# A two-layer gated network behind chunked attention on one core: some loads spread out, some stores moved from SP's queue to POOL's

## The chip, the cores and the metric

The kernel runs on one core of a Trainium2 chip. The metric is the device time of one execution in microseconds (us); the median of the timed runs counts. TensorE (PE) multiplies, VectorE (DVE), ScalarE (ACT) and GpSimd (POOL) work on tiles in SBUF, and SyncE (SP) issues DMA transfers. POOL and ACT can issue transfers too. Each engine takes its instructions strictly in the order of the program, and an instruction whose operand isn't there holds up all that stand behind it on that engine.

## What is computed

Attention over chunks of 64 tokens (8 batches, 8 heads, 576 tokens, 64 per head), whose result is laid out as x with 4608 tokens of 512, and then two gated layers with weights of 512 x 1536, 512 x 1536 and 1536 x 512; the second normalises its input first.

```python
def _moe_ref(x, w_gate, w_val, w_out):
    g = x @ w_gate
    silu = g * (1.0 / (1.0 + np.exp(-g)))
    val = x @ w_val
    return (silu * val @ w_out).astype(np.float32)

def _moe2_ref(x, w_gate, w_val, w_out, rms_g):
    rms = np.sqrt(np.mean(x * x, axis=-1, keepdims=True) + 1e-06)
    xn = x / rms * rms_g
    ...                          # then as above, on xn
```

## The kernel before

**Precision.** Every factor is split into a high part and a low rest, and a product is three matmuls: high by high, high by low, low by high (`mm3`, L641). The weights come as 64-bit numbers and are turned to 32 bits on ACT and DVE.

**Plain blocks.** The first layer's first 2560 tokens go through in five blocks of 512 (`emit_g`, `emit_v`, `emit_y`, j = 0 to 4), each in 12 iterations f over the hidden width; (j, f) names one. In block j the chunks run upwards or downwards by turns, so that the last three of a block are the first of the next. An iteration is 12 matmuls of g, 12 of v and 12 of the y of the iteration before. The weights' high parts stay in SBUF, their low parts don't: all but a few are stored to `lo1_d` in block 0, and blocks 1 to 4 load them again, `load_lo` (L193, tile l, 512 KB, g and v together, three slots) two iterations ahead and `load_lo_o` (L200, tile lo, 256 KB).

**Positions.** An iteration has three positions, numbered through from block 0; (j, f) begins at 36 j + 3 f. `put` (L805) hangs a step on a position and `spread` (L808) cuts a list of transfers into n nearly equal pieces on n positions in a row. On the positions hang the attention of the next tokens (tile i from position `score_at(i)` on; POOL normalises p, `att_n` L533, then DVE transposes it, `att_td` L541), the loads of q and k in 13 groups of 32 small transfers (`load_qk` L352; DVE transposes a piece of them in `trans_att` L457), the first layer's weight sums (`whole`, `first_add`, `first_keep`, L268 to L301: POOL adds in block 1 to 4, SP stores to `w1_d`) and the second layer's weight products (`comb_add`, `comb_cast`, `comb_rest`, `comb_keep`, L216 to L256: POOL and ACT work, SP stores to `w2_d`). `later2` names the ten of the 18 products that are made only in the tail.

**The tail.** From the end of block 4 on, seven stages s of up to 2 x 512 tokens (s = 0 and 1 the first layer's last 2048 tokens, s = 2 to 6 the second layer) use a scheme of seven products for a 2 x 2 block product. A stage is a gv stretch (6 x 14 products, six matmuls each) and a y stretch (42 products, six matmuls each). Their weights pass through a ring of 16 slots in SBUF: `load_ring` (L952) issues loads up to a number, each as soon as its slot is free. In s = 0 and 1 the ring tiles with k > 2 are loaded as one full number; `ring_split` (L973) makes the high part on ACT (L982) and the low on DVE or POOL (L985). The first ring loads are issued inside block 4, `load_ring(4)` at the start of (4, 8) and `load_ring(16)` at the start of (4, 9), ahead of what these iterations load themselves.

**Queues.** SP issues all transfers but eight, in program order: a load of l stands behind every q, k, v, weight, store and ring transfer that the program names before it.

Of the kernel before, what the change touches and what calls it, by code (L numbers as in the profile page):

```python
# [9 lines left out]
F32 = mybir.dt.float32  # L10
# [9 lines left out]
def tile_kernel(  # L20
# [14 lines left out]
    lo1_d: bass.AP,  # L35
    w1_d: bass.AP,
    x1_d: bass.AP,
    out: bass.AP,
):
    nc = tc.nc  # L40
# [44 lines left out]
    NB = TAIL // NW  # L85
# [94 lines left out]
    def chunk(j, f):  # L180
        return f if j % 2 == 0 else NF - 1 - f
# [68 lines left out]
    def comb_keep(nm, fp, k):  # L250
        z = SLOT[k]
        w = comb[1, nm, fp]["w", z // 2]
        a = z - z % 2
        nc.sync.dma_start(
            out=w2_d["gvo".index(nm), fp, :, a:z + 1], in_=w[:, :z - a + 1].bitcast(F32)
        )  # L256

# [37 lines left out]
        nc.gpsimd.tensor_tensor(out=t[which], in0=a, in1=b, op=op)  # L295

    def first_keep(nm, p, side):
        nc.sync.dma_start(
            out=w1_d["gvo".index(nm), p, :, 3 + 2 * side:5 + 2 * side],
            in_=flat[0, nm, 2 * p + side].rearrange("p (k f) -> p k f", k=2),  # L300
        )  # L301

    def place(nm, k):
        return {3: 6, 5: 4 if nm == "o" else 5, 4: 3, 6: 5 if nm == "o" else 4}[k]
# [29 lines left out]
    groups = [list(range(0, 2 * EARLY - 2)), list(range(2 * EARLY - 2, 2 * EARLY))]  # L334
# [122 lines left out]
    def trans_att(i):  # L457
        ts_ = []
        for z, nm in enumerate("qk"):
            t = att.tile([P, HP, P], F32, tag=f"{nm}T", name=f"{nm}T{i}")  # L460
            tv = t.rearrange("p a (b c) -> p a b c", c=32)
            (g0, n0), (g1, n1) = where[2 * i], where[2 * i + 1]
            if g0 == g1:
                nc.vector.transpose(out=tv, in_=gt[g0][z][:, :, 2 * n0:2 * n0 + 4, :])
            else:
                nc.vector.transpose(out=tv[:, :, 0:2], in_=gt[g0][z][:, :, 2 * n0:2 * n0 + 2, :])
                nc.vector.transpose(out=tv[:, :, 2:4], in_=gt[g1][z][:, :, 2 * n1:2 * n1 + 2, :])
            ts_.append([t[:, hp] for hp in range(HP)])
        qkT[i] = ts_
# [335 lines left out]
    def put(l, j, pos, fn):  # L805
        at.setdefault((l * NB + j) * NP + pos, []).append(fn)
# [12 lines left out]
    def score_at(i):  # L819
        return NP + 9 * (i - 8) // 2  # L820

    turned = {}
    for i in range(NW // P, NT_):
        j = order[i] * P // NW
        if i >= 8:
            a = score_at(i)
            m_, t_, n_, d0, d1 = ((1, 2, 3, 6, 8), (1, 3, 3, 5, 7))[i % 2]
            if i == 8:
                put(0, 0, a - 1, lambda: trans_att(8))
            put(0, 0, a, lambda i=i: att_both(i))  # L830
            put(0, 0, a + m_, lambda i=i: att_m(i))
            if i + 1 < NT_:
                put(0, 0, a + t_, lambda i=i: trans_att(i + 1))
                turned[i + 1] = a + t_
            put(0, 0, a + n_, lambda i=i: att_n(i))
            put(0, 0, a + d0, lambda i=i: att_td(i, 0))
            put(0, 0, a + d1, lambda i=i: att_td(i, 1))
            e = score_at(i + 2)
            if i + 2 >= NT_:
                put(0, 0, e, lambda i=i: att_both(i + 2))  # L840
            put(0, 0, e + 1, lambda i=i, j=j: att_lo(i, j))
        else:
            b = 9 * (i - 4)
            late = i == 4
            put(0, 0, b + (2, 1, 0, 0)[i - 4], lambda i=i: trans_tok(i))
            put(0, 0, b + 2 + late, lambda i=i: att_s(i))
            put(0, 0, b + 3 + late, lambda i=i: att_m(i))
            put(0, 0, b + 4 + late, lambda i=i: att_n(i))
            put(0, 0, b + 6 + late, lambda i=i: att_t(i))
            put(0, 0, b + 7 + late, lambda i=i, j=j: att_pv(i, j))  # L850
            put(0, 0, b + 8 + late, lambda i=i, j=j: att_lo(i, j))
        for c in (2 * i, 2 * i + 1):
            g = where[c][0]
            if g > 0 and c == groups[g][-1] and g + 2 < len(groups):
                if i > 8:
                    dq, nq = turned[i] + 1, 7
                else:
                    dq, nq = {4: (20, 9), 6: (29, 8), 8: (38, 7)}[i]
                spread(0, 0, dq, nq, lambda g=g: load_qk(g + 2))
    for j in range(1, NB):  # L860
        pj = j - 1
# [23 lines left out]
    w2 = [(nm, f) for nm, fp in pairs2[:8] for f in (fp, fp + NP2)]  # L885
    later2 = pairs2[8:]
# [24 lines left out]
    for j, p, nm in w1_at:  # L911
        a = 3 * min(chunk(j, 2 * p), chunk(j, 2 * p + 1)) + (3 if nm == "o" else 0)
# [39 lines left out]
    def load_ring(n):  # L952
        nonlocal wnext
        while wnext < min(n, len(wseq)):
            s, m, fp, k = wseq[wnext]
            t = wraw.tile([P, 2, HK], F32R, tag=RING[wnext % len(RING)], name=f"wr{m}{fp}_{k}_{s}")
            z = "gvo".index(m)
            if s >= NS:
                nc.sync.dma_start(out=t.bitcast(F32), in_=w2_d[z, fp, :, SLOT[k]])
            elif k > 2:  # L960
                nc.sync.dma_start(out=t[:, 1].bitcast(F32), in_=w1_d[z, fp, :, place(m, k)])
            else:
                side, c = PLAIN[m][k]
                nc.sync.dma_start(out=t[:, 0].bitcast(F32), in_=w1_d[z, fp, :, k])
                nc.sync.dma_start(
                    out=t[:, 1].bitcast(F32), in_=lo1_d[2 * fp + side, :, z, c * HK:(c + 1) * HK]
                )
            wt[s, m, fp, k] = t
            wnext += 1

    wsn = [0, 0]

    def ring_split(n):  # L973
        for z in range(2):
            while wsn[z] < min(n + 2 - 2 * z, wnext, len(wseq)):
                s, m, fp, k = wseq[wsn[z]]
                wsn[z] += 1
                if s >= NS or k < 3:
                    continue
                t = wt[s, m, fp, k]  # L980
                if z == 0:
                    nc.scalar.copy(t[:, 0], t[:, 1].bitcast(F32))  # L982
                else:
                    eng = nc.gpsimd if wsn[z] > 36 and m == "v" else nc.vector
                    eng.tensor_sub(t[:, 1], t[:, 1].bitcast(F32), t[:, 0].bitcast(F32))  # L985

    xo = {}
    xf = {}
# [395 lines left out]
    with tc.manual_schedule():  # L1384
        nc.vector.memset(ones.bitcast(F32), 1.0)
        make_identity(nc, ident)
        w1 = [(nm, f) for f in range(NF) for nm in "gvo"]
# [102 lines left out]
        for n, (l, j, f) in enumerate(iters):  # L1490
            def run(p):
                for fn in at.get(3 * n + p, ()):
                    fn()
                for kt, op in XFIRST.get(3 * f + p, ()) if j == NB - 1 else ():
                    xops[kt][op]()

            head = (l, j) == (0, 0)
            if (j, f) == (1, 0):
                conv.close()
                cv = open_pool(conv, "cv2", 2, "right")  # L1500
            if (j, f) == (NB - 1, 8):
                conv.close()
                attn.close()
                X2 = open_pool(two, "x2", 1, "right")
                for kt in range(2):
                    x_load(0, kt)
                    xops[kt] = x_prep(0, kt)
            if (j, f) == (NB - 1, 8):
                load_ring(4)

            if head and f == 0:
                pre_w1(8)
                issue(later)
                pre_w1(9)
                issue(load_tok(5))
            if head and f == 4:
                nc.sync.dma_start(out=rg, in_=moe2_rms_g.rearrange("(c p) -> p c", p=P))
            if head and f in (2, 5):
                issue(load_tok(6 + f // 5))
            if (j, f) == (NB - 1, 9):  # L1520
                load_ring(16)
            if prev is not None:
                lo()
            sg, product = emit_g(l, j, f)
            run(0)
            if head:
                conv1(3 * f + 4 if f else 2)
            v_product, lo = emit_v(l, j, f, sg)
            product()
            run(1)  # L1530
            if head and f == 0:
                conv1(3)
                conv1(4)
            elif head:
                conv1(3 * f + 5)
            if prev is not None:
                emit_y(*prev)
            v_product()
            if prev is not None and prev[2] == NF - 1:
                evac_y(*prev[:2])  # L1540
            run(2)
            if head:
                if not f:
                    conv1(5)
                conv1(3 * f + 6)
            prev = (l, j, f)
# [40 lines left out]
        for s in range(len(SB)):  # L1587
# [39 lines left out]
            for n in range(0, len(items), 2):  # L1627
                kk, fp = items[n]
# [62 lines left out]
```

## Time and profile before

| | us |
|---|---|
| three timed runs: median (lowest to highest) | 1735.5 (1734.0 to 1736.37) |
| the profiled execution | 1733.73 |
| its span, first to last instruction | 1731.8 |
| PE busy in it | 1695.7 (98%) |
| DVE, ACT, POOL busy | 1200.8, 865.8, 519.1 |
| the five plain blocks end at | 594.7 |
| the tail s = 0, 1, 2 begins at | 594.7, 771.6, 949.1 |

Busy times are of one profiled execution. Matmuls overlap in their pipeline, so a busy PE isn't a PE at its best pace; a stage's length against that of a like stage tells more. A line of waits names the engine and the line that stood idle, and what ended it. SPq is SP's queue: its instructions are issues, and the time of one is not that of the transfer.

### The profile page before, as it was taken

To read this page: it belongs to the slowest core of one execution; us is meant where nothing else is said; L and a number is where in the kernel's file an instruction comes from. 1 tells how busy PE (TensorE), PEld (TensorE's weight loads), DVE (VectorE), ACT (ScalarE), POOL (GpSimd) and SP (SyncE) were. 2 spreads that over 40 slices of the span, in tenths; PEclk is the share of its full clock that TensorE was granted. 3 is DMA by queue.
4 is the path that set the end of the run, shared out by engine and by line. 5 is a ranking of instruction groups with operands and counts; after the bars stand their busy time and mean duration, and the time that the engine had idled before them with its cause. 6 is when DMAs were issued, how large, how long until landed. Compare 5 with 4: busy or idle time off the path is not lost.

```text
span 1731.8 us, 29672 instructions
## 1 busy us (share of the span) xinstructions
PE 1695.7 (98%) x9870; PEld 1431.2 (83%) x9870; DVE 1200.8 (69%) x1936; ACT 865.8 (50%) x2044; POOL 519.1 (30%) x513
## 2 busy tenths in 40 slices
PE   7999999999999999999999999999999999999998
PEld 5788887877788788878887888888888888999998
DVE  6996767866664687896889477833783477358356
ACT  6774544545443466665665455433543354345343
POOL 1004657657563347227723541000000000000000
PEclk9999999999999999999999999999999999999999
DMA  9997888878888678746775799886788678989986
GB/s 237 321 256 171 212 217 246 215 210 247 210 263 284 197 223 282 228 138 218 239 241 157 244 322 307 223 215 194 239 223 215 194 230 230 272 271 284 278 253 175
DMA packets 486806, 405.98 MB, mean 234 GB/s; under 512 B 279552, under 2 KB 362752, under 8 KB 486656
## 3 DMA queue, kind: packets, MB, share of 16 engines
q1 hardware_dynamic: 483456, 403.71, 80.2%
q8 instruction: 79, 1.29, 0.3%
q10 hardware_dynamic: 3200, 0.39, 0.1%
q14 instruction: 71, 0.58, 0.1%
HBM read 321.91 MB, written 82.05 MB: 233 GB/s over the span
## 4 chain that ended last, share of the span: by engine, by line
PE 79%; DMA 7%; DVE 7%; SPq 3%; issue 1%; ACT 1%; POOL 1%; DVEq 0%; POOLq 0%; ACTq 0%
DMA l<-lo_scratch 2%; PE g L644 2%; SPq L453 2%; PE g L642 2%; PE g L643 2%; PE v L642 2%; PE ygA L643 2%; PE yvA L643 2%; PE yvA L644 2%; PE ygA L644 2%; PE yvA L642 2%; PE ygA L642 2%; PE v L643 2%; PE v L644 2%; DVE hp L1162 1%
## 5 line engine op out<-in xcount | busy, mean ns | idle before, releaser
L1126 POOL TENSOR_TENSOR h<-h,h 128x512 f32<-128x512 f32 (+1 forms) x42 | 56.7, 1351 | 661.5 <-DVE h L1104 661.5
L1162 DVE TENSOR_TENSOR hp<-h,hp 128x512 fp32r<-128x512 f32 (+1 forms) x252 | 164.6, 678 | 23.8 <-ACT hp L1161 18.6
L1161 ACT CAST hp<-h 128x512 fp32r<-128x512 f32 (+1 forms) x252 | 140.8, 589 | 41.2 <-PE yvA L644 13.0
L1085 ACT ACTIVATE sgt<-sgt 128x512 f32<-128x512 f32 (+1 forms) x126 | 75.9, 602 | 162.2 <-DVE sgt L1092 162.1
L644 PE MATMUL g<-xh,l 128*128 128x512 f32 x240 | 96.5, 402 | 14.9 <-DMA l<-lo_scratch 14.8
L535 POOL TENSOR_TENSOR p<-p,r 128x512 f32<-128x512 f32 x36 | 40.9, 1137 | 213.4 <-DVE r L534 177.6
L1104 DVE TENSOR_TENSOR h<-h,sgt 128x512 f32<-128x512 f32 (+1 forms) x126 | 89.1, 707 | 15.4 <-ACT sgt L1085 3.2
L642 PE MATMUL g<-xh,wg 128*128 128x512 f32 x240 | 95.5, 398 | 1.6 <-ACT xh L616 1.0
L642 PE MATMUL v<-xh,wv 128*128 128x512 f32 x240 | 96.3, 401 | 0.7 <-ACT wo L167 0.7
L643 PE MATMUL g<-xl,wg 128*128 128x512 f32 x240 | 95.2, 397 | 0.4 <-DVE xl L636 0.4
L644 PE MATMUL v<-xh,l 128*128 128x512 f32 x240 | 94.1, 392 | 0.0
L643 PE MATMUL v<-xl,wv 128*128 128x512 f32 x240 | 94.0, 392 | 0.0
L654 ACT ACTIVATE sg<-g 128x512 f32<-128x512 f32 x60 | 35.8, 596 | 92.4 <-PE g L644 91.8
L655 DVE SCALAR_TENSOR_TENSOR sg<-sg,g 128x512 f32<-128x512 f32 x60 | 41.0, 683 | 55.3 <-ACT sg L654 54.8
L644 PEld LDWEIGHTS g<-xh,l 128*128 128x128 f32 x240 | 46.1, 192 | 28.3 <-DMA l<-lo_scratch 18.4
L507 ACT ACTIVATE p<-both,m 128x64 f32<-128x64 f32 x224 | 66.7, 323 | 1.1
L643 PE MATMUL ygA<-hp,wro 128*128 128x512 f32 (+1 forms) x168 | 63.2, 376 | 0.4 <-DVE hp L1162 0.4
L642 PE MATMUL ygA<-hp,wro 128*128 128x512 f32 (+1 forms) x168 | 63.0, 375 | 0.4 <-ACT s3g L1078 0.4
L642 PE MATMUL yvA<-hp,wro 128*128 128x512 f32 (+1 forms) x168 | 62.8, 374 | 0.0
L644 PE MATMUL ygA<-hp,wro 128*128 128x512 f32 (+1 forms) x168 | 62.7, 373 | 0.0
L643 PE MATMUL yvA<-hp,wro 128*128 128x512 f32 (+1 forms) x168 | 62.7, 373 | 0.0
L644 PE MATMUL yvA<-hp,wro 128*128 128x512 f32 (+1 forms) x168 | 62.7, 373 | 0.0
(846 smaller groups left out, 5465.9 us busy)
## 6 DMA issues: line engine op xcount, KB each, us to landing
wrg<-w_scratch SPq DMA_DIRECT2D x210, 256.0 KB, 3.2
wrv<-w_scratch SPq DMA_DIRECT2D x210, 256.0 KB, 3.1
wro<-w_scratch SPq DMA_DIRECT2D x210, 256.0 KB, 3.4
l<-lo_scratch SPq DMA_DIRECT2D x36, 512.0 KB, 5.7
wrg<-w_scratch SPq DMA_DIRECT2D x84, 128.0 KB, 3.1
wrv<-w_scratch SPq DMA_DIRECT2D x84, 128.0 KB, 3.1
wro<-w_scratch SPq DMA_DIRECT2D x84, 128.0 KB, 2.4
lo<-lo_scratch SPq DMA_DIRECT2D x40, 256.0 KB, 4.5
```

What stands on the lines that cost most here:

```text
L507: nc.scalar.activation(pt[:, hp, x], s3[:, x, hp], AF.Exp, scale=SCALE, bias=m[:, x, hp:hp + 1], accum_out=r[:, 2 * hp + x],)
L535: nc.gpsimd.tensor_tensor(out=p8, in0=p8, in1=r.to_broadcast([P, HP * 2, CH]), op=ALU.mult)
L642: nc.tensor.matmul(o, sh, mh, start=first, stop=False, skip_group_check=free)
L643: nc.tensor.matmul(o, sh, ml, start=False, stop=False, skip_group_check=free)
L644: nc.tensor.matmul(o, sl, mh, start=False, stop=last, skip_group_check=free)
L654: nc.scalar.activation(sg[:, :n], g[:, :n], AF.Tanh, scale=0.5)
L655: return sg, lambda: nc.vector.scalar_tensor_tensor(out=sg[:, :n], in0=sg[:, :n], scalar=1.0, in1=g[:, :n], op0=ALU.add, op1=ALU.mult)
L1085: nc.scalar.activation(t[:, :tw], src[:, :tw], AF.Silu)
L1104: nc.vector.tensor_mul(h[:, :tw], src[:, :tw], sgt[pos][:, :tw])
L1126: nc.gpsimd.tensor_sub(a, a, b)
L1161: nc.scalar.copy(hh[:, :tw], src)
L1162: nc.vector.tensor_sub(hl[:, :tw], src, hh[:, :tw].bitcast(F32))
```

## The change

- `comb_keep` stores of the eight products made in the plain blocks are issued by POOL; those in `later2` stay with SP. `first_keep` stores are all issued by POOL. Together 32 + 36 transfers.
- The loads of q and k: where a group's pieces lay on 7 positions, they lie on up to 10, as far as the first transpose that reads them allows (9 groups; those at 48, 89 and 129 keep 7); the group at 38 begins at 37 and takes 8.
- `load_ring` in block 4 goes to 6, 11 and 16 at the start of (4, 9), (4, 10) and (4, 11).
- A new scratch `l1_d` in DRAM: in s = 0 the low halves of w_out's tiles with k > 2, which DVE has just made, are stored by SP, two calls of `ring_split` later; in s = 1 SP loads them beside the full numbers, and DVE's 24 subtractions fall away.

```diff
 def comb_keep(nm, fp, k):
-        nc.sync.dma_start(
+        queue = nc.sync if (nm, fp) in later2 else nc.gpsimd
+        queue.dma_start(
             out=w2_d["gvo".index(nm), fp, :, a:z + 1], in_=w[:, :z - a + 1].bitcast(F32)
 def first_keep(nm, p, side):
-        nc.sync.dma_start(
+        nc.gpsimd.dma_start(
...
+    STEPS = ((1, 2, 3, 6, 8), (1, 3, 3, 5, 7))
+    def turned_at(i):
+        return score_at(i - 1) + STEPS[(i - 1) % 2][1]
...
                 if i > 8:
-                    dq, nq = turned[i] + 1, 7
+                    first = groups[g + 2][0] // 2
+                    dq = turned_at(i) + 1
+                    nq = min(10, turned_at(first) - dq - 1)
                 else:
-                    dq, nq = {4: (20, 9), 6: (29, 8), 8: (38, 7)}[i]
+                    dq, nq = {4: (20, 9), 6: (29, 8), 8: (37, 8)}[i]
...
             elif k > 2:
-                nc.sync.dma_start(out=t[:, 1].bitcast(F32), in_=w1_d[z, fp, :, place(m, k)])
+                kept = s and m == "o"
+                nc.sync.dma_start(out=t[:, 0 if kept else 1].bitcast(F32), in_=w1_d[z, fp, :, place(m, k)])
+                if kept:
+                    nc.sync.dma_start(out=t[:, 1].bitcast(F32), in_=l1_d[fp, :, place(m, k) - 3])
...
     def ring_split(n):
+        now = lows[:]
+        lows.clear()
+        for age, dst, src in now:
+            if age:
+                nc.sync.dma_start(out=dst, in_=src)
+            else:
+                lows.append((1, dst, src))
...
+                kept = s and m == "o"
                 if z == 0:
-                    nc.scalar.copy(t[:, 0], t[:, 1].bitcast(F32))
-                else:
+                    nc.scalar.copy(t[:, 0], t[:, 0 if kept else 1].bitcast(F32))
+                elif not kept:
                     eng = nc.gpsimd if wsn[z] > 36 and m == "v" else nc.vector
                     eng.tensor_sub(t[:, 1], t[:, 1].bitcast(F32), t[:, 0].bitcast(F32))
+                    if m == "o":
+                        lows.append((0, l1_d[fp, :, place(m, k) - 3], t[:, 1].bitcast(F32)))
...
-            if (j, f) == (NB - 1, 8):
-                load_ring(4)
+            if j == NB - 1 and f >= 9:
+                load_ring((6, 11, 16)[f - 9])
...
-            if (j, f) == (NB - 1, 9):
-                load_ring(16)
```

## Rows read from the trace of the kernel before

**Rows 1.** Stages (from:to length): PE, PEld, DVE, ACT, POOL busy (count), clock, DMA share, GB/s.

```profile
138.10:246.10 108.00, 108.00 (x883) 88.08 (x882) 77.57 (x130) 54.35 (x201) 63.55 (x66) 1.00 0.82 202
246.10:361.20 115.10, 109.83 (x947) 88.91 (x946) 81.73 (x134) 56.46 (x208) 70.95 (x75) 1.00 0.85 225
361.20:482.00 120.80, 113.99 (x948) 90.83 (x947) 82.07 (x138) 57.26 (x210) 72.84 (x78) 0.97 0.82 217
482.00:594.70 112.70, 108.55 (x755) 88.10 (x754) 65.08 (x100) 44.73 (x134) 46.96 (x46) 0.97 0.82 264
...
888.50:949.10 60.60, 59.13 (x254) 46.73 (x253) 57.03 (x101) 38.69 (x81) 14.23 (x5) 1.00 0.53 157
...
1064.30:1121.50 57.20, 57.20 (x254) 47.36 (x253) 52.02 (x84) 30.56 (x55) 1.68 (x1) 1.00 0.81 230
```

**Rows 2.** Who PE waited for: 246 to 595 us, block 2, block 3 (total, times, longest).

```profile
PE g L644 <- DMA l<-lo_scratch: 14.8, 6, 4.1
...
PE g L644 <- DMA l<-lo_scratch: 4.6, 2, 3.6
...
PE g L644 <- DMA l<-lo_scratch: 6.0, 3, 3.3
```

**Rows 3.** PE in order of time around iteration (4, 11): start, length in us.

```profile
578.11 0.39 PE L642 MATMUL y_b<-hh,wo 128*128 128x512 f32 x1
...
579.47 0.39 PE L642 MATMUL g<-xh,wg 128*128 128x512 f32 x1
...
584.23 0.79 PE L644 MATMUL g<-xh,l 128*128 128x512 f32 x1 [4.14 <-DMA l<-lo_scratch]
...
588.66 0.63 PE L642 MATMUL v<-xh,wv 128*128 128x512 f32 x1
...
592.01 0.39 PE L642 MATMUL y<-hh,wo 128*128 128x512 f32 x1
```

**Rows 4.** SP's issues in order of time, 397 to 417 us: first, moved stores, last.

```profile
398.36 0.81 SPq L453 DMA_DIRECT2D xk<-in_k_dram  x2
...
402.22 0.52 SPq L254 DMA_DIRECT2D w_scratch<-wsg  x1
...
403.31 1.31 SPq L298 DMA_DIRECT2D w_scratch<-wao  x2
...
412.69 0.39 SPq L254 DMA_DIRECT2D w_scratch<-wsg  x1
...
416.12 0.50 SPq L197 DMA_DIRECT2D l<-lo_scratch  x1
```

**Rows 5.** The moved stores in blocks 2 and 3: count, ns min/median/max of an issue.

```profile
L254 SPq DMA_DIRECT2D w_scratch<-wsg x20: 332/408/1377, 250.0 to 459.6; - x20
...
L298 SPq DMA_DIRECT2D w_scratch<-wao x12: 376/393/1598, 250.5 to 467.6; - x12
L298 SPq DMA_DIRECT2D w_scratch<-wav x6: 350/376/523, 308.9 to 375.9; - x6
L298 SPq DMA_DIRECT2D w_scratch<-wag x4: 376/414/1262, 291.8 to 358.8; - x4
```

**Rows 6.** Issue to landing of the l loads in blocks 2 and 3.

```profile
DMA to landing us min/median/max: 4.4/5.8/9.3
```

**Rows 7.** SP's issues in order of time, first and last ring issue of 27.

```profile
561.54 0.32 SPq L964 DMA_DIRECT2D wrg<-w_scratch  x1
...
576.42 0.43 SPq L965 DMA_DIRECT2D wrv<-lo_scratch  x1
```

**Rows 8.** DVE's subtractions of w_out's low halves, s = 1's y stretch.

```profile
L985 DVE TENSOR_TENSOR wro<-wro x24: 412/416/1436, 895.4 to 945.3; 128x256 fp32r<-128x256 f32 x24
```

**Rows 9.** POOL normalising p, and who waited for it (138 to 595 us).

```profile
L535 POOL TENSOR_TENSOR p<-p,r x17: 1041/1045/1441, 243.6 to 478.8; 128x512 f32<-128x512 f32 x17
...
DVE pT L547 <- POOL p L535: 2.9, 1, 2.9
```

**Rows 10.** What ACT waited for, 138 to 595 us.

```profile
ACT wsg L242 <- DMA w_scratch<-wsg: 25.8, 8, 5.3
```

More of the change, by code (lines that the diff above doesn't have):

```diff
@@ L37, in tile_kernel @@
     x1_d: bass.AP,
+    l1_d: bass.AP,
     out: bass.AP,
@@ L820, in score_at @@
         return NP + 9 * (i - 8) // 2
-    turned = {}
+    STEPS = ((1, 2, 3, 6, 8), (1, 3, 3, 5, 7))
+    def turned_at(i):
+        return score_at(i - 1) + STEPS[(i - 1) % 2][1]
     for i in range(NW // P, NT_):
@@ L826, in tile_kernel @@
             a = score_at(i)
-            m_, t_, n_, d0, d1 = ((1, 2, 3, 6, 8), (1, 3, 3, 5, 7))[i % 2]
+            m_, t_, n_, d0, d1 = STEPS[i % 2]
             if i == 8:
@@ L833, in tile_kernel @@
                 put(0, 0, a + t_, lambda i=i: trans_att(i + 1))
-                turned[i + 1] = a + t_
             put(0, 0, a + n_, lambda i=i: att_n(i))
@@ L971, in tile_kernel @@
     wsn = [0, 0]
+    lows = []
     def ring_split(n):
+        now = lows[:]
[5 more added lines that the diff above has]
+                lows.append((1, dst, src))
         for z in range(2):
@@ L1681 @@
             w1 = dp.tile([3, 6, 128, 7, 256], F32, name="w1_scratch")
+            l1 = dp.tile([6, 128, 4, 256], F32, name="l1_scratch")
             x1 = dp.tile([512, 2048], F32, name="x1_scratch")
@@ L1686 @@
                 outs.append(nc.dram_tensor(f"out_{i}_dram", shape, dt, kind="ExternalOutput").ap())
-            tile_kernel(tc, *args, xn, w2, lo1, w1, x1, *outs)
+            tile_kernel(tc, *args, xn, w2, lo1, w1, x1, l1, *outs)
     r = _run(nc, [arrays], core_ids=[0])
```

## The prediction, made before the result was known

> **What bounds the kernel now.** The page's busy table comes first; it only says that TensorE (PE) leads by far, so a change can win no more than what PE loses in some stage. The second view, the table by stage, says where [rows 1]. The three middle plain blocks hold the same matmuls (block 1 two small attention groups fewer), yet take 108.0, 115.1 and 120.8 us: blocks 2 and 3 lose up to 7.1 + 12.8 = 19.9 us against block 1. The y stretch of a tail stage takes 60.6 us for s = 1 and 57.2 for s = 2: 3.4 us lost. From s = 2 on PE is busy all of the stretch, and nothing is to be had.
>
> The third view, who PE waited for from block 2 to the end of block 4, gives one name: the load of a low half, l<-lo_scratch, 14.8 us in 6 waits; 4.6 of it lie in block 2 and 6.0 in block 3 [rows 2]. The fourth, PE in order of time, shows what one such wait costs. In iteration (4, 11) the third matmul of g came 4.14 us late, and from it on a matmul took (588.66 - 584.23) / 10 = 0.44 us where (579.47 - 578.11) / 6 = 0.227 is usual: while PE stood, its granted clock had fallen from 2.4 to 1.2 GHz. The twelve matmuls of g ran 9.19 us instead of 2.72, those of v 3.35 instead of 2.72, so this wait cost 6.5 + 0.6 = **7.1 us** [rows 3]. Blocks 2 and 3 lose 4.6 + 6.0 = 10.6 us in the other waits, and block 3's granted clock of 0.97 adds 0.03 x 120.8 = 3.6: **14.2 us** that have a name, of the 19.9 by difference.
>
> Why is the load late? SP issues nearly every transfer, in the order of the program. Up to the l load before the worst wait of block 3 (3.3 us) SP made 30 issues without a rest, from 398.36 to 416.62: 18.3 / 30 = 0.61 us each [rows 4], against medians of 0.38 to 0.41 for one issue [rows 5]. The l load reached its turn at 416.12 and needs 5.8 us to land, the median [rows 6]. So the queue in front of it was long. Of the 30 issues, 4 are stores that now go to POOL and 21 are pieces of q and k.
>
> **The change part by part.**
>
> (1) *Stores to POOL.* 32 stores of weight products and 36 of first-layer sums leave SP; in blocks 2 and 3 these are 20 + 22 = 42 [rows 5], and 42 x 0.61 = 26 us of SP's queue. If every wait of PE goes, SP has 14 to 20 us less for the rest; 26 is more, so the queue is looser than now even with PE at full pace. Before the worst wait it is 4 x 0.61 = 2.4 us.
>
> (2) *q and k pieces over 10 positions.* A group is 32 issues. At position 121, where the l load of (3, 6) is issued, the group that starts at 116 had put out 6/7 of them (27) and will have put out 6/10 (19): 8 x 0.61 = 4.9 us earlier, with (1) 7.3 us against a wait of 3.3. For (2, 4), position 79, it is 22 against 16, 3.7 us, and stores on top, against a wait of 3.6. Only the group at 129 keeps its 7 positions in block 3, so (3, 10) and (3, 11) get the stores alone; at 42 in 236 us some four in the 22 us before, 2.4 us, against waits of 2.7 together. Something is left there. The pieces end later, but by the table of positions still 3 positions (9 us) or more ahead of the transpose that reads them, where the groups that stay have 2.
>
> Of the 14.2 us with a name (19.9 at most) I take **14** back: what (3, 11) and a wait or two on the edge keep, I set against the part of the 19.9 that has no name. Ends: 6, if bursts in the queue remain, and 19.9.
>
> (3) *Ring loads in steps 6, 11, 16.* Until now 8 ring issues in (4, 8) and 16 in (4, 9) stood ahead of the l load of (4, 11); now 10 do. SP made 27 issues, ring and others, from 561.54 to 576.85, 0.57 each [rows 7]: 14 fewer are 7.9 us, against a wait of 4.1. The wait goes, and the clock's fall with it: **7.1 us**. Ring tiles 11 to 15 will be issued near 578; the first is read 11 tiles of 6 x 0.227 us after the tail's start, at 594.7 + 15 = 610: nothing becomes late there.
>
> (4) *Low halves of w_out kept for s = 1.* In s = 1's y stretch 24 subtractions of 0.416 us go [rows 8], 10 us of DVE's 57.0 in 60.6 [rows 1]. DVE has no reserve there, so I take **2.4** of the 3.4 back; ends 0 and 3.4. For it SP issues 24 stores of 128 KB in s = 0 and 24 more loads in s = 1. The y stretch uses the DMA engines at 0.53 [rows 1] and ring loads run 16 tiles, 22 us, ahead, so they cost nothing; with that cover gone 48 x 0.4 = 19 us.
>
> (5) *What POOL pays.* No row shows POOL issuing a transfer. The nearest are SP's issues of the same stores, 0.33 to 1.6 us [rows 5], and POOL's own instruction over a 128x512 tile, 1.04 [rows 9]. I take 1.0, since it is POOL that has to carry it out. POOL is free for 115.1 - 71.0 + 120.8 - 72.8 = 92 us in blocks 2 and 3 [rows 1]; 42 us fit. The stores stand on POOL behind the tensor ops that made their data, so they wait for little. Behind them stands the normalising of p, which DVE transposes next; that has once been thin, DVE waited 2.9 us for p [rows 9]. I charge **1.5 us**; ends -1 (a gain, since ACT waited 25.8 us for stores to free their buffer, and they leave earlier [rows 10]) and 4.
>
> **Sum:** 14 + 7.1 + 2.4 - 1.5 = 22.0 us. The profiled execution took 1733.7 us (span 1731.8), so one like it would take 1711.7. It was 1.8 faster than the median of the three timed runs, 1735.5; the median comes to **1713.5**.
>
> **The rivals.** *B: the transfers are late, not the queue.* The DMA engines are busy 0.85 and 0.82 of blocks 2 and 3 [rows 1]. If the l loads wait for them, the moved stores still fly on the same engines and the 14 us shrink. For it speaks that an issue took 0.61 us where 0.4 is usual; against it, that block 1, with a share of 0.82, loses nothing. Parts (3) and (4) remain: 7.1 + 2.4 - 1.5 = 8.0, **1727.5**; with some of the 14, down to 1721. The Trainium skill, page "DMA: Bandwidth & Descriptors", section "Issuing engines are not separate DMA queues", states this rival as a rule: transfers started by any engine run on the same 16 DMA engines and interleave, and several issuers save only the time of issuing. By that page part (1) would free 42 x 0.4 = 17 us of SP's queue and not 26, an estimate.
>
> *C: POOL becomes the late engine (slower).* Place: the normalising of p in blocks 2 and 3. POOL's price X for a store decides: 92 us for 42 stores are 2.2 us each; above that POOL falls behind, p comes late, DVE stands at its transposes and PE at the scores. The kernel is slower than before once 42 x (X - 2.2) > 23.5, X = 2.76; at X = 3 it takes 1735.5 - 23.5 + 34 = **1746**. Against it: SP's longest issue of such a store is 1.6 us [rows 5].
>
> *D: no gain.* The l loads are late because their slots come free late, and what one load gains the next loses: 1735, within 0.2%. Against it: SP had no rest ahead of the worst wait [rows 4].
>
> **How the numbers follow.** Forecast 0.58 (own range 1706 to 1721), B 0.24 (1721 to 1731), C 0.08, D 0.07, and 0.03 for more than the forecast (all 19.9 come back). The range 1705 to 1731 holds the forecast and B, some 0.8. A measurement of this kernel tells 0.2%, 3.5 us, from no change: faster 0.58 + 0.24 + 0.03 = 0.85, same 0.07, slower 0.08.
>
> **What would show it.** Right: blocks 2 and 3 near 109 us each; PE waiting under 3 us for l loads; no half clock in (4, 11); s = 1's y stretch near 58 us; POOL's issues near 1 us. Wrong: l loads late with SP at rest (D); l loads landing later than 5.8 us after their issue (B); DVE waiting for p (C); DVE's transposes of q and k waiting for their pieces, which would say that (2) went too far.

## The result, and the profile after

| | before | after |
|---|---|---|
| timed runs: median (lowest to highest), us | 1735.9 (1734.0 to 1739.9), 4 runs | 1706.3 (1705.5 to 1709.1), 4 runs |
| the profiled execution, and its span | 1733.7, 1731.8 | 1709.1, 1707.3 |
| PE waiting for l loads in blocks 2 to 4 | 14.8, 6 times | 2.6, once |
| POOL busy | 519.1 | 549.8 |

The changed kernel is faster by 29.6 us: the ratio is 0.983, 95% interval 0.981 to 0.985. Two of all the timed runs below took far longer than their fellows (3426.9 us, part (4) alone; 4359.2 us, the stores of x on ACT) and are in no median here (with its one the latter's is 1718.4). The changed kernel's stages, as in [rows 1] (from:to length; PE, PEld, DVE, ACT, POOL busy; clock, DMA share, GB/s): blocks 1 to 4, then the y stretches of s = 1 and s = 2.

```profile
137.72:245.77 108.05, 108.05 (x883) 88.13 (x882) 78.07 (x130) 54.24 (x201) 71.00 (x81) 1.00 0.80 206
245.77:354.76 108.99, 108.99 (x948) 89.06 (x946) 86.87 (x134) 56.23 (x208) 82.03 (x96) 1.00 0.90 243
354.76:468.30 113.54, 110.91 (x948) 90.13 (x946) 88.12 (x138) 58.62 (x213) 83.12 (x99) 0.98 0.90 230
468.30:573.74 105.44, 105.44 (x756) 86.26 (x754) 68.16 (x99) 42.26 (x128) 52.40 (x58) 1.00 0.85 273
...
867.12:924.24 57.12, 57.12 (x253) 47.33 (x252) 52.93 (x77) 38.40 (x81) 14.50 (x8) 1.00 0.73 222
1039.50:1096.62 57.12, 57.12 (x254) 47.33 (x252) 51.93 (x84) 30.56 (x55) 1.67 (x1) 1.00 0.82 230
```

Against [rows 1]: blocks 2 and 3 fall from 235.9 to 222.5 (13.4 less), block 4 from 112.7 to 105.4 (7.3), s = 1's y stretch from 60.6 to 57.1 (3.5). That is 24.2 of the 24.5 us between the two spans. In block 2, block 4 and both y stretches PE is now busy from end to end; only block 3 still loses something. One line of the waits from 246 to 595 us says what (total, times, longest), and PE in order of time says where (start, length):

```profile
PE g L646 <- DMA l<-lo_scratch: 2.6, 1, 2.6
```

```profile
455.81 0.39 PE L645 MATMUL g<-xl,wg 128*128 128x512 f32 x1
458.83 0.50 PE L646 MATMUL g<-xh,l 128*128 128x512 f32 x1 [2.63 <-DMA l<-lo_scratch]
...
459.93 0.63 PE L644 MATMUL g<-xh,wg 128*128 128x512 f32 x1
...
462.49 0.63 PE L644 MATMUL v<-xh,wv 128*128 128x512 f32 x1
462.92 0.51 PE L645 MATMUL v<-xl,wv 128*128 128x512 f32 x1
463.27 0.39 PE L646 MATMUL v<-xh,l 128*128 128x512 f32 x1
```

This is iteration (3, 11): a wait of 2.6 us, and behind it 3 us in which matmuls follow each other at 0.43 us: from 459.90 to 462.90 the granted clock is 0.50, which is 1.2 GHz, until 2.4 GHz is back. It is the pattern of [rows 3], which itself is gone from (4, 11). POOL's issues of the moved stores in blocks 2 and 3 (count; ns min/median/max):

```profile
L256 POOL DMA_DIRECT2D w_scratch<-wsg x19: 537/577/608, 245.9 to 435.8; - x19
...
L300 POOL DMA_DIRECT2D w_scratch<-wao x11: 539/548/597, 245.3 to 442.8; - x11
```

### The profile page after: what moved, and what is told of

Read it like the earlier page. It is cut to its first block, busy times and chain, and to the rows that moved or that the text cites. A ratio compares the mean times of both kernels' runs of the same rounds, so it can differ in the third digit from the quotient of the medians.

```text
span 1707.3 us, 29702 instructions
## 1 busy us (share of the span) xinstructions
PE 1685.3 (99%) x9870; PEld 1428.5 (84%) x9870; DVE 1210.6 (71%) x1912; ACT 865.9 (51%) x2044; POOL 549.8 (32%) x581
## 4 chain that ended last, share of the span: by engine, by line
PE 92%; DVE 4%; DMA 2%; ACT 1%; issue 1%; SPq 0%; POOL 0%; DVEq 0%
PE v L644 3%; PE g L646 3%; PE g L644 3%; PE g L645 3%; PE v L645 3%; PE v L646 3%; PE yvA L645 2%; PE ygA L645 2%; PE yvA L646 2%; PE ygA L644 2%; PE yvA L644 2%; PE ygA L646 2%; PE y L644 2%; PE y L645 2%; PE y L646 1%; PE y_b L646 1%
## 5 line engine op out<-in xcount | busy, mean ns | idle before, releaser
L1147 POOL TENSOR_TENSOR h<-h,h 128x512 f32<-128x512 f32 (+1 forms) x42 | 56.7, 1351 | 661.5 <-DVE h L1125 661.5
L678 DVE TENSOR_TENSOR hl<-sg,hh 128x512 fp32r<-128x512 f32 x60 | 61.7, 1029 | 9.3 <-ACT hh L676 8.6
L676 ACT CAST hh<-sg 128x512 fp32r<-128x512 f32 x60 | 37.1, 618 | 54.8 <-DVE sg L673 54.8
L646 PE MATMUL yvA<-hp,wro 128*128 128x512 f32 (+1 forms) x168 | 62.8, 374 | 0.0
L644 PE MATMUL yvA<-hp,wro 128*128 128x512 f32 (+1 forms) x168 | 62.7, 373 | 0.0
```

What stands on the lines that cost most here:

```text
L644: nc.tensor.matmul(o, sh, mh, start=first, stop=False, skip_group_check=free)
L646: nc.tensor.matmul(o, sl, mh, start=False, stop=last, skip_group_check=free)
L678: return product, lambda: nc.vector.tensor_sub(hl[:, :n], sg[:, :n], hh[:, :n].bitcast(F32))
L1147: nc.gpsimd.tensor_sub(a, a, b)
```

## The experiments

Medians are of timed runs; each ratio is to runs of the kernel before beside it. Stages are of one profiled execution. A gain in us beside a ratio, for the four parts, is the ratio taken of 1734.3. 29 runs of the kernel before, beside the first four experiments, lay between 1730.1 and 1742.1, median 1734.3.

### The four parts, each alone in the kernel before

Part (1), the stores:

```diff
-        nc.sync.dma_start(
+        queue = nc.sync if (nm, fp) in later2 else nc.gpsimd
+        queue.dma_start(
...
-        nc.sync.dma_start(
+        nc.gpsimd.dma_start(
             out=w1_d["gvo".index(nm), p, :, 3 + 2 * side:5 + 2 * side],
```

> The kernel before with part (1) alone: 32 stores of weight products and 36 of first-layer sums issued by POOL, nothing else. Queue theory: 42 of them lie in blocks 2 and 3 and free 42 x 0.61 = 26 us of SP's queue there, against 14.2 us lost by name; I expect 8 to 12 us of these back (blocks 2 and 3 together 224 to 228 us instead of 235.9), the waits for l in (2, 4) and (3, 6) gone or under 1 us, and the half clock of (4, 11) unchanged, as no store stands there: faster by 6 to 12 us, about 1726. Rival B (the transfers are late on the DMA engines): the same bytes still move, so blocks 2 and 3 keep 233 us or more and the gain is under 3 us. Rival C: DVE waits longer for p and the time rises.

Measured: 1720.6, ratio 0.992 (0.990 to 0.994), **13.5 us faster**. Blocks 2 and 3, then issue to landing of their l loads:

```profile
245.50:355.31 109.81, 109.28 (x948) 88.91 (x946) 87.36 (x134) 56.42 (x208) 82.11 (x96) 1.00 0.86 236
355.31:470.60 115.29, 111.22 (x947) 90.03 (x946) 90.12 (x138) 58.96 (x213) 83.38 (x99) 0.99 0.87 229
```

```profile
DMA to landing us min/median/max: 4.1/5.9/7.6
```

225.1 us against 235.9, 10.8 less. The median l load takes as long to land as before (5.8, [rows 6]) with the DMA engines a little fuller; the loads come in time because they are issued earlier. That speaks for the queue and against rival B. Who PE waited for in the two blocks:

```profile
PE g L645 <- DMA l<-lo_scratch: 4.6, 3, 2.4
```

That is 4.6 us where it was 10.6 [rows 2]: 0.5 in (2, 4), as expected, but still 1.6 in (3, 6), and 2.4 in (3, 11). The gain is a little over the 6 to 12 us expected. Block 4 stays at 112.7, as expected.

Part (2), the spread of the q and k pieces:

```diff
-                    dq, nq = turned[i] + 1, 7
+                    first = groups[g + 2][0] // 2
+                    dq = turned_at(i) + 1
+                    nq = min(10, turned_at(first) - dq - 1)
```

> The kernel before with part (2) alone: a group of 32 q and k pieces over 10 positions in place of 7. By the prediction's working it takes 4.9 us out of the queue ahead of the l load of (3, 6) (wait 3.3) and 3.7 us ahead of (2, 4) (wait 3.6); (3, 10) and (3, 11) get nothing. Queue theory: both waits shrink to about 0 to 1, some 6 to 9 us of blocks 2 and 3 come back with the clock, 1727 to 1730. Rival B: spreading the same bytes over more time also thins the DMA engines, so this run alone does not speak against B; it does if e1 gains as much. Rival D: the waits move to the next l load and the gain is under 3.5 us.

Measured: 1729.6, ratio 0.997 (0.996 to 0.999), 5.2 us faster. Blocks 2 and 3, and who PE waited for in them:

```profile
245.62:359.40 113.78, 110.04 (x947) 88.94 (x946) 79.47 (x134) 56.74 (x208) 71.40 (x75) 1.00 0.84 227
359.40:477.45 118.05, 112.39 (x948) 89.72 (x946) 83.52 (x137) 57.73 (x210) 72.83 (x77) 0.99 0.85 220
```

```profile
PE g L644 <- DMA l<-lo_scratch: 9.4, 9, 2.4
```

231.8, 4.1 less. Expected were 6 to 9. The two waits that were aimed at did shrink, from 3.6 to 1.7 in (2, 4) and from 3.3 to 0.9 in (3, 6), but others came: where there were five in the two blocks, 10.6 us [rows 2], there are nine, 9.4 us, the longest of 2.4 in place of 3.6. Spreading turned a few deep waits into many small ones. Of the 4.1 us the waits give 1.2; the clock, 0.99 for 0.97 in block 3, is worth some 0.02 x 118 = 2.4 by estimate.

Part (3), the ring loads:

```diff
-            if (j, f) == (NB - 1, 8):
-                load_ring(4)
+            if j == NB - 1 and f >= 9:
+                load_ring((6, 11, 16)[f - 9])
...
-            if (j, f) == (NB - 1, 9):
-                load_ring(16)
```

> The kernel before with part (3) alone: ring tiles in steps 6, 11, 16 at f = 9, 10, 11 of block 4. Queue theory: the wait of 4.1 us in (4, 11) and the half clock behind it go, block 4 falls from 112.7 to about 105.6, nothing else moves: faster by 7.1 us, about 1728.5. If the wait only moves to the first ring tiles of the tail, block 4 falls and the first tail stage grows from 176.9 by as much: no gain.

Measured: 1730.2, ratio 0.997 (0.996 to 0.999), 4.7 us faster. Block 4:

```profile
481.01:587.40 106.39, 105.74 (x756) 86.35 (x755) 64.61 (x99) 43.27 (x131) 46.97 (x46) 1.00 0.88 282
```

6.3 us less than in [rows 1], at a clock of 1.00. The first tail stage is as long as before (177.0 against 176.9), so nothing was handed on. The expectation was 7.1.

Part (4), the kept low halves:

```diff
-                nc.sync.dma_start(out=t[:, 1].bitcast(F32), in_=w1_d[z, fp, :, place(m, k)])
+                kept = s and m == "o"
+                nc.sync.dma_start(out=t[:, 0 if kept else 1].bitcast(F32), in_=w1_d[z, fp, :, place(m, k)])
+                if kept:
+                    nc.sync.dma_start(out=t[:, 1].bitcast(F32), in_=l1_d[fp, :, place(m, k) - 3])
```

> The kernel before with part (4) alone: the low halves of w_out, worked out in s = 0, are stored and read back in s = 1. Prediction: the y stretch of s = 1 falls from 60.6 to 57.2 to 58.2 us, all else stays: faster by 2.4 to 3.4 us, 1732 to 1733. If the 48 added issues on SP have no cover, s = 0 or s = 1 grows elsewhere and the gain goes.

Measured: 1730.4, ratio 0.998 (0.996 to 0.999), 4.3 us faster. The y stretch of s = 1:

```profile
890.70:947.82 57.12, 57.12 (x254) 47.30 (x252) 52.90 (x77) 38.39 (x81) 14.48 (x8) 1.00 0.73 221
```

3.5 us less, all there was to lose. The 48 added issues on SP show nowhere: s = 0 takes 176.8, as before. The four gains alone, 13.5 + 5.2 + 4.7 + 4.3 = 27.7, make nearly the whole of 29.6. Each is good to some 3 us (the interval of its ratio), the sum to some 6, so no overlap of the parts shows, and a small one would not.

### What does part (1) relieve: SP's turns, bytes, or neither?

The changed kernel, each moved store issued twice by POOL; then the same with the second store cut to 64 bytes a partition:

```diff
+        if (nm, fp) not in later2:
+            queue.dma_start(
+                out=w2b_d["gvo".index(nm), fp, :, a:z + 1], in_=w[:, :z - a + 1].bitcast(F32)
+            )
```

> The changed kernel, with each moved store issued a second time by POOL, into scratch that nothing reads: 68 more POOL issues and as many more bytes of stores on the DMA engines, nothing more on SP. Queue theory: SP's queue is as in the changed kernel, so the time stays within 3 us of it (1706.3), with POOL busy 68 x 0.57 = 39 us more and the l loads landing a few tenths of a us later. Rival B (what counts is the load on the DMA engines): with 42 more stores in blocks 2 and 3 the waits for l return, blocks 2 and 3 grow to 230 us or more from 222.5 and the time is 1714 or more. Rival C: POOL has 68 us left in blocks 2 and 3 and 24 fit, no change.

Measured: 1738.8, slower than the kernel before (ratio 1.002, 1.001 to 1.004) and **32.5 us** slower than the changed one. The stores of `first_keep` are doubled in the same way. The queue theory, as I had put it, is wrong here. Blocks 2 and 3, and the landing of l:

```profile
246.54:368.38 121.84, 111.84 (x947) 89.96 (x946) 82.19 (x134) 56.88 (x208) 94.19 (x120) 0.97 0.97 288
368.38:494.48 126.10, 114.67 (x948) 91.36 (x946) 87.70 (x139) 58.78 (x213) 93.48 (x118) 0.96 0.95 267
```

```profile
DMA to landing us min/median/max: 4.2/5.7/10.7
```

With the DMA engines at 0.95 to 0.97 the median l load still lands in 5.7 us (5.4 in the changed kernel). The loads that PE waited for are in the main issued late: seven of them landed in 4.2 to 8.1 us, 6.05 on average, where the same seven took 5.41 in the changed kernel; one owes most of its wait to its landing (8.1 against 4.7). In order of time SP makes 312 issues in these blocks that take 198.9 us, 0.64 each; in the changed kernel it is 309 in 166.6, 0.54 each. 75 of them are longer than 0.7 us, against 41.

> The changed kernel, with the second issue of each moved store as in the run that doubled them (1738.8 us), but of 64 bytes a partition, 8 KB in all, in place of 256 or 512 KB: POOL issues as often as there, the DMA engines move hardly more than in the changed kernel. If the 32 us of the doubled stores came from their bytes (DMA share 0.96 and 0.95 in blocks 2 and 3 in place of 0.90 and 0.89, so that landings and SP's issues grow longer), this run is back at 1706 to 1710 with blocks 2 and 3 near 222.5. If they came from POOL's 68 more issues of 0.57 us, or from a second transfer as such, it stays near 1738.

Measured: 1711.0, ratio 0.986 (0.985 to 0.987). Blocks 2 and 3:

```profile
246.49:355.47 108.98, 108.98 (x947) 89.03 (x946) 81.77 (x134) 56.37 (x208) 95.35 (x120) 1.00 0.90 243
355.47:467.65 112.18, 109.62 (x947) 89.14 (x946) 88.58 (x139) 59.20 (x213) 95.59 (x118) 1.00 0.89 234
```

So 1738.8 - 1711.0 = 27.8 of the 32.5 us are the bytes, and at most 4.7 are POOL's 68 more issues. Only the bytes of the second stores differ between these two runs, and SP's mean issue in the two blocks is 0.64 us with them and 0.52 without, at DMA shares of 0.96 and 0.90. So the doubled bytes do cost, by lengthening SP's issues. Below that the two don't go in step (0.55 with the spread alone at 0.84 and 0.85, 0.52 here at 0.90), and what in a fuller DMA queue lengthens an issue isn't shown.

The counterpart: the stores whole on POOL, and SP gets its issues back, with hardly any bytes (the second store of 64 bytes, issued by SP; the edit is against the run before, and `first_keep` has the same):

```diff
-            queue.dma_start(
+            nc.sync.dma_start(
                 out=w2b_d["gvo".index(nm), fp, :, z, 0, :16], in_=w[:, z - a, 0, :16].bitcast(F32)
```

> The changed kernel, its moved stores whole on POOL, and with each of them a store of 64 bytes a partition, 8 KB in all, issued by SP at the same place of the program, into scratch that nothing reads. SP gets back its 68 issues, 42 of them in blocks 2 and 3, and their waits for POOL's data, but not their bytes; the DMA engines carry hardly more. What does part (1) relieve? If it is SP's turns: the gain of (1) goes, blocks 2 and 3 rise from 222.5 toward the 231.8 of the run with the spread alone, and the time toward 1706 + 9 = 1715. If it is the bytes of these stores among the transfers that SP has under way: blocks 2 and 3 stay at 218 to 223 and the time at 1706 to 1710. Between them, say 1711 to 1713, each has a share.

Measured: 1719.8, ratio 0.991 (0.989 to 0.992), 13.5 us slower than the changed kernel. Blocks 2 and 3:

```profile
245.04:360.86 115.82, 111.74 (x947) 90.33 (x946) 86.65 (x134) 56.73 (x208) 81.72 (x96) 0.99 0.87 234
360.86:476.78 115.92, 111.81 (x947) 89.91 (x946) 87.42 (x137) 58.55 (x213) 82.55 (x99) 0.99 0.88 229
```

```profile
PE g L656 <- DMA l<-lo_scratch: 7.4, 5, 2.8
```

231.7 us: what the spread alone left (231.8), in one profiled execution each. The gain of part (1) in these blocks is gone, though not one of the large stores went back to SP. The cleanest pair is this run and the one with the 64-byte stores on POOL: the same transfers and the same bytes, only their issuer differs, and it is 231.7 against 221.2 us in the two blocks and 1719.8 against 1711.0 in time. SP's issues there take 186.1 us, 354 of them, against 166.6; the 43 small stores hold SP for 20.9 us of issuing, and it stands some 4.8 us more at them, 1.3 of that for POOL's data. The l loads land in 5.7 us as ever. Part (1) relieves SP's turns. The bytes it leaves as they were.

### Does it have to be POOL?

The kernel before with the same stores issued by ACT (`first_keep` is shown, `comb_keep` has the same edit):

```diff
-        nc.sync.dma_start(
+        nc.scalar.dma_start(
             out=w1_d["gvo".index(nm), p, :, 3 + 2 * side:5 + 2 * side],
```

> The kernel before with part (1) alone, but the stores issued by ACT and not by POOL. ACT issues through a queue like SP's at 0.4 to 0.6 us each; SP's queue loses the same 42 issues in blocks 2 and 3. Queue theory: what counts is that SP is rid of them, so blocks 2 and 3 gain as with POOL (10.7 us, from 235.8 to 225.1), less what ACT's 42 x 0.5 = 21 us of issuing and its waits for POOL's data hold up the casts that PE reads. If POOL as issuer is what brought it (a path of its own to the DMA engines), this run stays near the kernel before, 1731 or more.

Measured: 1771.0, **slower than before by 2%** (ratio 1.021, 1.019 to 1.023). SP is rid of the stores here too, and yet blocks 1 to 3 take 123.3, 127.7 and 124.3 us, with the DMA engines at 0.71 to 0.77 only. PE waits for l loads, from 137 to 650 us:

```profile
PE g L645 <- DMA l<-lo_scratch: 33.3, 12, 5.0
```

They land as fast as ever, 5.4 us in the median of blocks 2 and 3, so they are issued late. SP's own waits, in blocks 2 and 3, tell why (total, times, longest):

```profile
SPq L454 <- DMA w_scratch<-wsg: 17.9, 9, 4.8
SPq L454 <- DMA w_scratch<-wav: 13.1, 4, 4.5
SPq L454 <- DMA w_scratch<-wao: 4.9, 3, 3.2
SPq L204 <- DMA w_scratch<-wsg: 4.8, 2, 2.8
...
SPq L197 <- DMA w_scratch<-wsg: 4.3, 1, 4.3
```

SP stands until stores that ACT issued have landed, 25 times and 56.7 us in the two blocks. Transfers of SP and ACT take eight completion semaphores in turn, as the trace's records name them, and the next transfer on a semaphore is not issued until the one before it on the same semaphore has landed. POOL's transfers take others. ACT issues a store only after its own work and after POOL's data; SP stops for it when it comes to the eighth transfer behind it in the program. That it is the shared semaphores that stop SP is read from these waits; no run separates it from ACT's lateness. The next run shows one such stop.

### The residue: the stores of x

SP also stands at the stores of x until ACT has written x. First, ACT issues them (in the changed kernel):

```diff
-            nc.sync.dma_start(out=x1_d[:, o:o + P].rearrange("(h p) t -> p h t", p=P), in_=t)
+            nc.scalar.dma_start(out=x1_d[:, o:o + P].rearrange("(h p) t -> p h t", p=P), in_=t)
```

> The changed kernel, with the 16 stores of x issued by ACT, which writes x, in place of SP. In the profile of the changed kernel SP stood 4.1 us (422.24 to 426.36) at such a store until ACT had written x, then issued without a rest up to the l load of (3, 11), at 452.02, which came 2.6 us late and took the clock down. Queue theory: without the 4.1 us that load is issued about 4 us earlier, the last wait for l goes, block 3 falls from 113.5 to 109, the time to 1702. If SP only meets its next wait earlier (a slot of lo or of q and k not free yet), the l load is as late as before and the time stays at 1706.

Measured: 1717.9, ratio 0.991 (0.988 to 0.993), 12 us slower than the changed kernel. SP's wait in blocks 2 and 3; then ACT's issue and the SP pieces behind it in order of time (start, length):

```profile
SPq L455 <- DMA x_scratch<-x: 26.7, 8, 5.9
```

```profile
249.87 0.37 ACTq L614 DMA_DIRECT2D x_scratch<-x  x1
```

```profile
247.32 8.69 SPq L455 DMA_DIRECT2D xq<-in_q_dram  x3
256.06 0.96 SPq L455 DMA_DIRECT2D xk<-in_k_dram  x2
```

Three small pieces stretch over 8.7 us: the third stood until the store, issued at 249.87, had landed at 255.69. Second, SP issues the store of x one position later:

```diff
+    x1_late = {}
+
     def att_lo(i, j):
+        if i in x1_late:
+            issue([x1_late.pop(i)])
```

> The changed kernel, with the 16 stores of x issued by SP one position (some 3 us) later, so that SP need not stand there until ACT has written x. Unlike the run in which ACT issued them (1718.4 us: there SP stood 23.5 us in 7 places in blocks 2 and 3 until such a store had landed, seven of SP's own issues further on), nothing else changes hands. In the changed kernel SP stood 8.7 us in blocks 2 and 3 for ACT, 4.1 of it some 26 us ahead of the l load that is 2.6 us late. If the queue's length at that load is what counts, its wait goes, block 3 falls from 113.5 to 109 and the time to 1702. If the freed time is lost again at the next slot that isn't free, or in fuller DMA engines, 1706 or more.

Measured: 1706.7, ratio 0.983 (0.982 to 0.985): the time of the changed kernel. Blocks 2 and 3:

```profile
247.17:356.15 108.98, 108.98 (x947) 89.04 (x946) 89.82 (x134) 56.23 (x208) 82.59 (x96) 1.00 0.89 244
356.15:465.14 108.99, 108.99 (x947) 89.03 (x946) 88.38 (x138) 58.65 (x213) 82.17 (x99) 1.00 0.91 237
```

In the profile the last wait for l is gone and block 3 is as short as block 2, 4.5 us less; the timed runs show no gain (the expectation was 1702). The profiled execution of the changed kernel was the slowest of its four (1709.1; the others 1705.5 to 1706.3), so (3, 11) may be late in some executions only. That stays open.

### How much POOL can carry

```diff
+    def pool_work():
+        for _ in range(4):
+            nc.gpsimd.tensor_tensor(out=idle, in0=idle, in1=idle, op=ALU.add)
...
+        pool_work()
         nc.gpsimd.dma_start(
```

> The changed kernel, with four additions over an unused 128x128 tile on POOL ahead of each moved store, so that a store costs POOL its 0.57 us and about 2.4 us on top (a 128x256 operation on POOL takes 0.8 to 0.9). Rival C's rule: POOL has 92 us free in blocks 2 and 3, 42 stores at 3.0 us need 126, so it is 34 us late and the time is about 1706 + 34 = 1740, with DVE waiting for p. If POOL's lateness counts earlier than by its total, because a row of such stores stands right ahead of the normalising of p, more than that. If the rule is wrong and POOL is off every path there, no change: 1706 to 1710.

Measured: 1759.6, ratio 1.015 (1.012 to 1.017), 53 us slower than the changed kernel. The additions; whom DVE waited for from 137 to 645 us; blocks 2 and 3:

```profile
L254 POOL TENSOR_TENSOR idle<-idle 128x128 f32<-128x128 f32 x272 | 129.0, 474 | 16.4
```

```profile
DVE pT L557 <- POOL p L545: 31.9, 7, 7.9
```

```profile
246.74:376.77 130.03, 115.48 (x947) 91.48 (x946) 82.35 (x136) 56.92 (x209) 120.14 (x187) 0.96 0.76 204
376.77:501.13 124.36, 114.21 (x948) 89.94 (x946) 85.29 (x131) 56.59 (x209) 118.36 (x176) 0.97 0.79 205
```

A store now cost POOL 0.57 + 4 x 0.474 = 2.47 us. DVE waits for p, as rival C had it (2.3 us in the changed kernel). But PE hardly stands at the scores then (0.6 us), as C went on; in blocks 2 and 3 its longest waits are others:

```profile
PE g L652 <- DVE sg L665: 10.0, 7, 3.7
PE ssq L761 <- POOL al L750: 7.1, 2, 5.6
```

The first is DVE, late with a tile whose buffer PE's next g needs, the second POOL's own tile `al`, with which PE sums the squares for the second layer's normalising. By C's rule POOL should be 42 x (2.47 - 2.2) = 11 us late in blocks 2 and 3; they are 254.4 - 222.5 = 31.9 us longer. With one addition in place of four:

> The changed kernel, with one addition over an unused 128x128 tile on POOL ahead of each moved store (474 ns each in the run with four of them, which took 1759.6), so that a store costs POOL 0.57 + 0.47 = 1.04 us, the price that the prediction took for it. If POOL has a reserve up to some price and is late above it, this run is at 1706 to 1708 and the prediction's 1.5 us for POOL were too many by that much. If POOL's time counts from the first us, in proportion to the run with four, it is at 1706 + 53 / 4 = 1719.

Measured: 1709.9, ratio 0.986 (0.984 to 0.987), 3.6 us over the changed kernel, with intervals that overlap, so at most a small loss. The profiled execution, the fastest of its four (1706.6), doesn't show where it lies: blocks 2 and 3 take 219.1 us there. A store cost POOL 0.57 + 0.51 = 1.08 us here. From 137 to 465 us PE waited:

```profile
PE g L654 <- DMA l<-lo_scratch: 0.8, 1, 0.8
PE both L608 <- DVE pT L563: 0.6, 1, 0.6
```

The second line, in block 1, is new against the changed kernel; the run with the 64-byte stores on POOL, 4.7 us over, has it too. So POOL's time is nearly free at about 1 us a store and dear at 2.5; where between them it turns, no run shows.

## Why the prediction was right, and where it was off

**The place.** Right in each stage: blocks 2 and 3, (4, 11), s = 1's y stretch, and nothing else. The forecast for the profile was 22.0 us, the spans differ by 24.5.

**(1) and (2) together, 14 forecast, 13.4 measured**, 10.8 and 4.1 alone. The mechanism was right: with the turns given back, the gain went. The 26 us that were to leave SP's queue were too many. The moved stores took SP 23.3 us of issuing in the two blocks; all its issues there fell from 183.3 us to 166.6 in the changed kernel and to 162.8 with part (1) alone, 17 to 21 us less, nearer to the 17 that the prediction worked out beside it. The 0.61 us a store was taken from a burst in which SP did not issue without a rest: of its 18.3 us, 15.8 are issues (0.53 each) and 2.5 are gaps and waits. The forecast of 14 did not suffer by it, as it was bounded by what PE lost and not by the 26. "Something is left there" for (3, 10) and (3, 11) came true at (3, 11). The step on (2) was too generous for (2) alone: it set issues saved ahead of one l load against the wait there, 3.7 and 4.9 us against 3.6 and 3.3, and expected both waits to go. They fell to 1.7 and 0.9, and the lateness showed at seven other loads (nine waits of 9.4 us in all).

**(3) 7.1 forecast, 7.3 measured** in the changed kernel, where the moved stores of block 4 are in it too, and 6.3 alone (4.7 in time): the wait and the fall of the clock behind it, added up from [rows 3], both came back, and no ring tile was late. Its 0.57 us a ring issue, too, is not all issuing: of the 15.3 us of [rows 7], 10.7 are issues (0.40 each) and 4.1 are SP standing for a transfer of its own to land.

**(4) 2.4 forecast, 3.5 measured.** The mis-sized term: I held back 1.0 because DVE had no reserve, 57.0 busy in 60.6 [rows 1]. With 10 us of subtractions gone DVE is busy 52.9 in 57.1, and PE waits for nothing there. The whole difference from s = 2 was to be had.

**(5) -1.5 forecast, nothing visible.** The step that failed is the price X: 1.0 us a store, taken from POOL's arithmetic on a tile of 128x512 [rows 9]; the issue took 0.55 to 0.58 and hardly depends on size. SP's issues of the same stores, 0.38 to 0.41 [rows 5], were the nearer row. At the price I took, the run with one addition lost 3.6 us or, by the intervals, next to nothing; whether the charge fitted its price stays open.

**From profile to median.** The sum was carried over as if the profiled execution of the changed kernel, too, lay 1.8 us below its median. It lay 2.8 above, and with the fourth timed run the one of before lay 2.2 below: 1733.7 - 1709.1 = 24.6, and 24.6 + 2.2 + 2.8 = 29.6. With 22.0 forecast, the gain missed by 7.6 us: 2.6 are mis-sized steps, (4) and (5) above all, and 5.0 are this offset. Which execution the profiler took is luck, and two thirds of the miss with it.

**Rival B** named the wrong place: its 14 us came back with the same bytes on the same engines, and the l loads land no faster (5.4 us against 5.8, and 5.9 with part (1) alone). But what it rests on is real: doubled stores cost 27.8 us by their bytes. With them the two theories meet: SP's issues are longer (0.64 us for 0.52), SP's queue falls behind, the l load is issued late. The rule of the Trainium skill, page "DMA: Bandwidth & Descriptors", section "Issuing engines are not separate DMA queues", that another issuer saves only the time of issuing, agrees with the trace. The run that gave SP its issues back shows that this is what part (1) saved here, and that it was worth 9.2 us in blocks 2 and 3.

**Rival C** had the first link of the chain right (DVE waits for p), not the last (PE waited for sg and for POOL's al, hardly at the scores), and too late a point. Free time summed over a block, 92 us, isn't reserve: while DVE waited 31.9 us for p, POOL was still idle for some 16 us of the two blocks (120.1 busy of 130.0, 118.4 of 124.4). That its work is due at certain times, and what is free behind it doesn't help, is how I read it. At X = 2.47 the kernel was 24.8 us slower than before (1759.6 against 1734.8 beside it), where the rule gave 2.76 for break-even.

**Rival D** falls for part (1), where waits that went did not come back at the next load. For part (2) alone it holds in good part: there the waits were shared out, 10.6 us to 9.4.

## What to carry to other kernels

When loads come late, look at the queue that issues them before the engines that carry them: issue times in order, the mean of one issue, and how long a load needs from issue to landing, which here stayed at 5.4 to 5.9 us while its waits went from 10.6 us to 2.6 or to 19.0. Before a transfer is moved to another engine, ask on whose data that engine waits and whose semaphores its transfers share: the same stores gained 13.5 us on POOL and lost 36.2 on ACT (1771.0 against 1734.8 beside it). An engine's free time is a reserve only up to the first due date in it; test it with dummy work of a known length.

## What the runs showed of the hardware that was not expected

- A transfer of 256 or 512 KB costs POOL 0.55 to 0.58 us to issue, with a spread of some 70 ns in blocks 2 and 3, where SP's issues of the same stores go up to 1.6 us [rows 5]. A store of 8 KB costs it as much (537 to 552 ns in the run with the 64-byte stores).
- In blocks 2 and 3 SP stood 25 times before and 19 times after, each over 0.15 us, for a transfer of its own to land, 14.9 and 14.5 us in all, and each time it was the eighth before the one that waited. No such wait was for a transfer that POOL issued. Whether more than eight could be under way with another use of semaphores, the runs don't tell.
- DVE's subtraction for hl took 929 ns on average before and 1107 after. In order of time, 17 of 49 lie beside no work of POOL and take 668, 18 lie beside POOL's arithmetic and take 1148, and 14 lie beside a store that POOL issues and take 1587. In the two runs with twice as many POOL issues the mean is 943 and 926, so what makes it long is open. PE does not wait for hl in the changed kernel.
